# Six score banks instead of four on VectorE in three quads, 128-wide weight reads for B, and B's input transposed in 512-token pieces, in a two-branch attention kernel

## The chip, the cores and the metric

The kernel runs on one core of one Trainium2 chip. Times are device microseconds of that core, given as the median of several executions. Before the change the kernel took 463.41 us (three runs, 463.3 to 463.55). "Faster" or "slower" needs 2%, which is 9.3 us here. Smaller differences are read from ratios with 95% intervals and from the traces.

## The reference

Two attention layers over 2048 tokens of width 448 (16 heads of 28) are computed and set side by side.

```python
def _A_ref(x, wq, wk, wv, wo):            # 16 heads of q, one shared head of k and v
    q = (x @ wq).reshape(B, S, H, Dh).transpose(0, 2, 1, 3)
    k = x @ wk
    v = x @ wv
    scores = einsum("bhqd,bkd->bhqk", q, k) * (Dh ** -0.5)
    p = softmax(scores)
    o = einsum("bhqk,bkd->bhqd", p, v)
    return o.transpose(0, 2, 1, 3).reshape(B, S, H * Dh) @ wo

def _B_ref(x, wqkv, wo):                  # every token sees itself and 7 earlier ones, 2 apart
    # ... q, k, v from x @ wqkv; W, dil = 8, 2
    logits = where(mask, einsum("bhsd,bhswd->bhsw", q, kg) * scale, -1e9)
    o = einsum("bhsw,bhswd->bhsd", softmax(logits), vg)
    return o.transpose(0, 2, 1, 3).reshape(B, S, D) @ wo

return concatenate([a, b], axis=-1)
```

A has 16 x 2048 x 2048 = 67 million exponentials, B next to none. A sets the time, and B's work has to fit beside it.

## The kernel before

A's scores come in 1024 tiles of 128 x 512, each filling one PSUM bank. Sixteen *quads* of 64 tiles follow one another. Two slots of banks take turns: one of three tiles, one of two. ScalarE takes the exponential of a whole slot at once (1536 or 1024 columns). In the quads listed in `OFF_AT`, four rounds of the three-tile slot give their third tile to VectorE, which evicts it and computes the exponential by a polynomial in three passes over two tiles at a time.

```python
SLOTS = ((0, 1, 2), (3, 4))
OFF_AT = {q: (0, 2, 5, 7) for q in range(1, 16)}
OFF_AT.update({q: (0, 1, 3, 4, 6, 7, 9, 10) for q in ()})
# ...
            off = g.offload(n, us)
            na = len(us) - off
            w = 512 * na
            x = a("act", t_exp(w), lambda e, b0=b0, w=w, n=n: e.activation(
                g.expT[:, n % ERING, 0:w], g.ps[:, 512 * b0:512 * b0 + w], ACT.Exp, scale=SCALE),
              R=[("ring", slot)], W=[("expT", n % ERING)], pr=-50)
# ...
    def d_exp(self, bank, slot):
        # ... the eviction, one per tile
        o = a("dve", t_dve_ps(512), lambda e: e.tensor_scalar(
            out=xx[:, 512 * h:512 * h + 512], in0=g.bank(bank), scalar1=-128.0 * A2, scalar2=128.0 * (129 + EOFF),
            op0=ALU.mult, op1=ALU.add), R=[("ring", slot)], W=[("d_x", m % 2, h)], pr=-45)
        # ... then, per two tiles, three scalar_tensor_tensor passes with pr=-0.5
```

`a(engine, duration, emit, R=reads, W=writes, pr=priority, rel=earliest)` only registers an operation. A list scheduler then fixes each engine's order from the registered durations, so a small edit can reorder every engine. The loads that the change touches:

```python
        a("act", 0.5, ...xst <- A_x[0:512]..., W=["xst"], pr=-21)          # first 512 tokens of x, cut here
        a("act", 1.1, wload(g.wk, g.A_wk, 0, DH), W=["wk"], dsem="i_wk", land=3, pr=-20, ninc=2)
        a("sp", 1.1, wload(g.wq, g.A_wq, 0, KC), ..., W=[("wq", 0)], dsem="i_wq0", land=3, pr=-25, ninc=2)
        for c in range(1, NCH):
            for t in range(4):
                a("sp", 1.25, one(lambda e, c=c, t=t: e.dma_start(
                    out=g.xT_A[:, t, 512 * c:512 * c + 512], in_=g.A_x[0, 512 * c:512 * c + 512, XB0[t]:XB0[t] + 128],
                    transpose=True)), W=[("xT", c, t)], dsem=f"i_xa{c}.{t}", land=4.6, pr=-20 + c)
        for t in range(4):
            a("sp", 3.5, one(lambda e, t=t: e.dma_start(
                out=g.xT_B[:, t, :], in_=g.B_x[0, :, XB0[t]:XB0[t] + 128], transpose=True)),
              W=[("xT_B", t)], dsem=f"i_xb{t}", land=8, pr=0, rel=4)
```

B's q and k are computed with weights read `KC` = 112 columns wide, and B's 512 transposing matmuls also take 112-wide operands:

```python
                        g.bank(u.bank, p1=KC), g.wqkv[:, kt, w * D + KC * t:w * D + KC * t + KC],
# ...
                    g.bank(u.bank, 128, 128 * t, p1=KC), g.prod2[:, w, KC * t:KC * t + KC], g.ident[:, :],
```

Of the kernel before, what the change touches and what calls it, by code (L numbers as in the profile page):

```python
# [39 lines left out]
OFF_AT.update({q: (0, 1, 3, 4, 6, 7, 9, 10) for q in ()})  # L40
LATE = 2
DR = 2
# [6 lines left out]
class Op:  # L49
    __slots__ = ("eng", "dur", "emit", "deps", "pr", "rel", "name", "use", "dsem", "land", "nd",  # L50
                 "kids", "start", "end", "seq", "waits", "signal", "count", "vc", "ninc", "claims", "idx",
                 "dense", "fill", "full", "opt", "alone", "lock", "ring", "tiled", "pv")

    def __init__(self, eng, dur, emit, pr, rel, name):
        self.eng, self.dur, self.emit, self.pr, self.rel, self.name = eng, dur, emit, pr, rel, name
        self.deps = set()
        self.use = None
        self.dsem = None
        self.land = 0.0
        self.ninc = 1  # L60
        self.kids = []
        self.start = self.end = None
        self.waits = []
        self.signal = False
        self.claims = None
        self.vc = None
        self.dense = 0.0
        self.fill = None
        self.full = 0
        self.opt = ()  # L70
        self.alone = True
        self.ring = False
        self.tiled = False
        self.pv = False
        self.lock = isinstance(dur, Lock) or (eng == "gp" and emit is not None)
# [16 lines left out]
class Sched:  # L92
# [49 lines left out]
    def run(self, engines):  # L142
# [44 lines left out]
        while left:  # L187
# [5 lines left out]
            if e == "dve":  # L193
                r1 = min((r for (r, o) in cand["dve"] if o.ring), default=None)
                if r1 is not None:
                    n = sum(1 for (_, o) in cand["act"] if o.ring)
                    limit = max(r1, H + (0.9 if n < 1 else 0) - self.QKT - 0.2 - 0.69)
# [33 lines left out]
            if best is None and e == "pe" and self.FILL and T > 4 and (nxt is None or nxt > T + 0.12) and area(T) < self.IDLE:  # L231
# [164 lines left out]
class Gen:  # L396
# [63 lines left out]
    def alloc(self, es):  # L460
# [12 lines left out]
        self.wqkv = sb([128, 4, 2 * D], BF16, "wqkv")  # L473
# [63 lines left out]
    def consts(self):  # L537
# [21 lines left out]
        a("gp", 0.8, lambda e: e.memset(g.wqkv[0:64, 3, :], 0.0), W=["wqkvz"], pr=-8.1)  # L559
# [21 lines left out]
    def loads(self):  # L581
# [11 lines left out]
        a("act", 1.1, wload(g.wk, g.A_wk, 0, DH), W=["wk"], dsem="i_wk", land=3, pr=-20, ninc=2)  # L593
        a("sp", 1.1, wload(g.wq, g.A_wq, 0, KC), R=[("d_x", 0, 0), ("d_x", 0, 1)], W=[("wq", 0)], dsem="i_wq0", land=3, pr=-25, ninc=2)
        a("gp", 1.5, wload(g.wv, g.A_wv, 0, DH), W=["wv"], dsem="i_wv", land=4, pr=-8.3, ninc=2)
        a("gp", 1.5, wload(g.wq, g.A_wq, KC, D), R=[("d_x", 0, 0), ("d_x", 0, 1)], W=[("wq", 1)], dsem="i_wq", land=4, pr=-7.5, ninc=2)
        for c in range(1, NCH):
            for t in range(4):
                a("sp", 1.25, one(lambda e, c=c, t=t: e.dma_start(
                    out=g.xT_A[:, t, 512 * c:512 * c + 512], in_=g.A_x[0, 512 * c:512 * c + 512, XB0[t]:XB0[t] + 128],  # L600
                    transpose=True)), W=[("xT", c, t)], dsem=f"i_xa{c}.{t}", land=4.6, pr=-20 + c)
        for t in range(4):
            a("sp", 3.5, one(lambda e, t=t: e.dma_start(
                out=g.xT_B[:, t, :], in_=g.B_x[0, :, XB0[t]:XB0[t] + 128], transpose=True)),
              W=[("xT_B", t)], dsem=f"i_xb{t}", land=8, pr=0, rel=4)
        a("sp", 1.2, lambda e: [
            e.dma_start(out=g.wqkv[:, 0:3, :], in_=g.B_wqkv[0:384, 0:2 * D].rearrange("(t p) c -> p t c", p=128)),
            e.dma_start(out=g.wqkv[64:128, 3, :], in_=g.B_wqkv[384:448, 0:2 * D]),
            ], W=["wqkv"], dsem="i_wb", land=8, pr=1, rel=4, ninc=2)
# [79 lines left out]
    def a_v(self, c):  # L689

        g, a = self, self.s.add
        pr = c + (0.9 if c else 1.3)
# [27 lines left out]
    def a_q(self, sc, first=False):  # L720
# [3 lines left out]
        for t in range(4):  # L724
            if first:
                pr, rel = (-9.5, 0) if t == 0 else (4.0 + 10 * t, 17.0)
# [28 lines left out]
    def a_loop(self):  # L755
# [6 lines left out]
        pair, late = [], []  # L762
        g.nd = 0
        g.quad = None
        n, pos = -1, 0
        while pos < NU:
# [40 lines left out]
            if off:  # L807
                pair.append((us[na],) + g.d_exp(b0 + na, slot) + (1,))
# [3 lines left out]
            while late and late[0][0] <= n // 2:  # L812
                for x in late.pop(0)[1]:
                    dqs[x[0][:2]][x[0][3]].append(x)
                    if all(dqs[x[0][:2]]):
                        g.pv_group([y.pop(0) for y in dqs[x[0][:2]]])
            for u in us:
                js = quads[u[:2]]
                while all(js):
                    g.pv_group([x.pop(0) for x in js])  # L820

    def pv_group(self, grp):
# [5 lines left out]
        def pv(e):  # L828
            order = [o.seq for o in all_pv]
            first, last = box[0].seq == min(order), box[0].seq == max(order)  # L830
            for (_, _, tb, j), _, src, w in grp:
                x = e.matmul(g.bank(PVBANK, p0=32 * j, p1=32 * j + 32), g.v_aug[:, w, tb, :], src,  # L832
# [9 lines left out]
        all_pv.append(o)  # L842
        if len(all_pv) == 16:
# [11 lines left out]
    def d_exp(self, bank, slot):  # L855
# [11 lines left out]
        o.ring = True  # L867
        if h:
# [4 lines left out]
                out=u, in0=lo, scalar=EP * F, in1=lo, op0=ALU.add, op1=ALU.mult), R=di, W=["d_u"], pr=-0.5)  # L873
            a("dve", t_dve_1x(1024), lambda e: e.scalar_tensor_tensor(  # L874
                out=v, in0=u, scalar=EQ * F * F, in1=lo, op0=ALU.add, op1=ALU.mult), R=["d_u"] + di, W=["d_u"], pr=-0.5)
            a("dve", t_dve_1x(1024), lambda e: e.scalar_tensor_tensor(  # L876
                out=out, in0=v, scalar=EL / F ** 3, in1=xx, op0=ALU.mult, op1=ALU.subtract),
              R=["d_u"] + di, W=[("dexp", m % DR)], pr=-0.5)
        return ("dexp", m % DR), out[:, 512 * h:512 * h + 512].bitcast(BF16)

    def a_quad_end(self, sc, t):
# [5 lines left out]
        for hf in range(hv):  # L887
# [7 lines left out]
            o.deps.update(g.pvs[sc, t])  # L895
# [37 lines left out]
    B0 = 30.0  # L933
# [14 lines left out]
    def b_qk(self, c):  # L948
        g, a = self, self.s.add
        T = g.B0 + g.BSTEP * 4 * c  # L950
        for t in range(4):
            for w in range(2):
# [4 lines left out]
                for kt in range(4):  # L957
                    a("pe", t_mm(512), lambda e, u=u, t=t, kt=kt, w=w: e.matmul(  # L958
                        g.bank(u.bank, p1=KC), g.wqkv[:, kt, w * D + KC * t:w * D + KC * t + KC],
                        g.xT_B[:, kt, 512 * c:512 * c + 512], start=kt == 0, stop=kt == 3),  # L960
                      R=[("xT_B", kt), "wqkv", "wqkvz"], W=[u], use=u, pr=pr, rel=rel, dense=512)
# [4 lines left out]
    def b_v(self, k):  # L966
# [5 lines left out]
        for kt in range(4):  # L972
# [3 lines left out]
              R=[("xT_B", kt), "wqv", "wqvz"], W=[u], use=u, pr=pr, rel=rel, dense=448)  # L976
# [141 lines left out]
```

## Time and profile before

| | before |
|---|---|
| time, median | 463.41 us |
| profiled span | 461.5 us |
| up to the first exponential | 10.94 us |
| first to last exponential | 443.61 us |
| after the last exponential | 6.95 us |
| exponentials on ScalarE | 264 of 1024 columns, 145 of 1536, one of 512 |
| granted clock | 1.00 |

The prediction below shows the busy table, the three stretches and the groups by shape. Four more lines come from the page's table of the costliest groups (line, engine, operation, tiles, shapes, count, then busy us and mean ns of one, then idle time before it and who ended it):

```profile
L800 ACT ACTIVATE expT<-ps 128x1024 bf16<-128x1024 f32 (+1 forms) x410 | 441.7, 1232 | 2.8 <-PE ps L783 2.4
...
L864 DVE TENSOR_SCALAR d_x<-ps 128x512 f32<-128x512 f32 x60 | 41.5, 691 | 39.0 <-PE ps L783 36.8
...
L1059 PE MATMUL ps<-ident,prod 128*112 128x128 bf16 x512 | 43.9, 225 | 0.0
...
L958 PE MATMUL ps<-xT_B,wqkv 128*112 128x512 bf16 x128 | 40.5, 398 | 0.1
```

### The profile page before, as it was taken

The numbers are of one execution on the slowest core, as the hardware profiler recorded it, in microseconds if no ns is written. First come the engines' busy times: TensorE is split into PE (matmuls) and PEld (weight loads), VectorE is DVE, ScalarE is ACT, GpSimd is POOL, SyncE is SP. The second block draws the span as 40 slices with busy tenths as digits, with TensorE's granted clock in tenths as the row PEclk, the third lists the DMA queues.
The fourth block names the chain that finished last, engine by engine and source line by source line (L and its number), as shares of the span: only waits on it lengthen the run. The fifth ranks groups of instructions, "written<-read, shape, count | busy, mean of one in ns | idle before, by whom it ended". The sixth has DMA issues, their size and how long they took to land.

```text
span 461.5 us, 8681 instructions
## 1 busy us (share of the span) xinstructions
PE 422.8 (92%) x3649; PEld 168.2 (36%) x3701; DVE 365.9 (79%) x607; ACT 447.3 (97%) x430; POOL 9.3 (2%) x28
## 2 busy tenths in 40 slices
PE   7889998999998999999989999999899998997995
PEld 2332332333542434334432443334343442443331
DVE  6447888989899796888888688898889878687853
ACT  3999999999999999999999999999999999999994
POOL 7000000000000000000000000000000000000000
PEclk9999999999999999999999999999999999999999
DMA  8991121000401220002201230002200330410001
GB/s 150 164 229 33 48 75 60 11 0 22 161 21 53 89 74 27 1 14 87 91 11 50 81 101 11 12 0 92 86 26 20 111 101 12 136 46 0 11 3 48
DMA packets 41718, 27.34 MB, mean 59 GB/s; under 512 B 17090, under 2 KB 41520, under 8 KB 41680
## 3 DMA queue, kind: packets, MB, share of 16 engines
q1 hardware_dynamic: 40080, 25.35, 19.5%
q0 software_dynamic: 304, 0.73, 0.9%
q10 hardware_dynamic: 1296, 0.71, 0.5%
q8 instruction: 29, 0.48, 0.4%
q14 instruction: 9, 0.07, 0.0%
HBM read 17.60 MB, written 5.52 MB: 50 GB/s over the span
## 4 chain that ended last, share of the span: by engine, by line
ACT 88%; PE 8%; DVE 1%; DMA 1%; issue 0%; ACTq 0%
ACT expT L800 88%; PE ps L783 2%; PE ps L832 1%; PE ps L958 1%; DMA wk<-in_A_wk_dram 1%; PE ps L973 1%; PE ps L781 1%; PE ps L733 1%; PE ps L1059 1%; ACT e_t L1034 0%; PE ps L662 0%; PE ps L917 0%; DVE kT L679 0%; PE ps L747 0%; DVE PV_T L893 0%
## 5 line engine op out<-in xcount | busy, mean ns | idle before, releaser
L800 ACT ACTIVATE expT<-ps 128x1024 bf16<-128x1024 f32 (+1 forms) x410 | 441.7, 1232 | 2.8 <-PE ps L783 2.4
L783 PE MATMUL ps<-qT,kT 32*128 32x512 bf16 x833 | 123.3, 384 | 16.2 <-ACT expT L800 12.9
L832 PE MATMUL ps<-expT,v_aug 128*32 128x512 bf16 x964 | 96.1, 389 | 0.1
L864 DVE TENSOR_SCALAR d_x<-ps 128x512 f32<-128x512 f32 x60 | 41.5, 691 | 39.0 <-PE ps L783 36.8
L783 PEld LDWEIGHTS ps<-qT,kT 32*128 32x128 bf16 x833 | 30.3, 91 | 94.5 <-ACT expT L800 75.3
L781 PE MATMUL ps<-qT,kz 128*128 128x512 bf16 x160 | 50.2, 382 | 10.7 <-ACT expT L800 8.3
L832 PEld LDWEIGHTS ps<-expT,v_aug 128*32 128x32 bf16 x964 | 24.6, 93 | 60.4 <-issue 57.7
L999 DVE TENSOR_TENSOR stage<-qTB,kTB 112x1024 bf16<-112x1024 bf16 x64 | 42.2, 679 | 2.7 <-PE ps L1008 2.7
L1059 PE MATMUL ps<-ident,prod 128*112 128x128 bf16 x512 | 43.9, 225 | 0.0
L1053 DVE TENSOR_TENSOR prod<-Vsh,a_n 128x896 bf16<-128x896 bf16 x64 | 37.8, 616 | 7.2 <-PE ps L1059 7.2
L958 PE MATMUL ps<-xT_B,wqkv 128*112 128x512 bf16 x128 | 40.5, 398 | 0.1
L1059 PEld LDWEIGHTS ps<-ident,prod 128*112 128x112 bf16 x512 | 34.4, 129 | 16.8 <-issue 14.1
L874 DVE SCALAR_TENSOR_TENSOR d_u<-d_u,d_x 128x1024 f32<-128x1024 f32 x30 | 36.4, 1215 | 0.0
L876 DVE SCALAR_TENSOR_TENSOR dexp<-d_u,d_x 128x1024 int16<-128x1024 f32 x30 | 36.4, 1214 | 0.0
L872 DVE SCALAR_TENSOR_TENSOR d_u<-d_x 128x1024 f32<-128x1024 uint16 x30 | 36.3, 1210 | 0.1
L1008 PEld LDWEIGHTS ps<-ones,stage 112*128 112x128 bf16 x512 | 19.4, 96 | 8.4 <-issue 3.2
L1008 PE MATMUL ps<-ones,stage 112*128 112x4 bf16 x512 | 22.1, 167 | 0.0
L781 PEld LDWEIGHTS ps<-qT,kz 128*128 128x128 bf16 x191 | 11.9, 97 | 25.2 <-ACT expT L800 23.1
L958 PEld LDWEIGHTS ps<-xT_B,wqkv 128*112 128x112 bf16 x128 | 14.1, 128 | 16.4 <-issue 11.1
L733 PE MATMUL ps<-xT_A,wq 128*128 128x512 bf16 x57 | 18.3, 383 | 0.6 <-issue 0.3
L1066 PE MATMUL ps<-wo_B,oT 112*128 112x448 bf16 x64 | 18.1, 356 | 0.2 <-DVE oT L1062 0.2
L408 PE MATMUL ps<-warm 128*128 128x512 bf16 x54 | 17.8, 384 | 0.2 <-issue 0.2
(102 smaller groups left out, 302.9 us busy)
## 6 DMA issues: line engine op xcount, KB each, us to landing
Vsh<-v_scratch SPq DMA_DIRECT2D x16, 896.0 KB, 4.7
v_scratch<-Vst SPq DMA_DIRECT2D x16, 112.0 KB, 1.7
out_dram<-outB SPq DMA_DIRECT2D x16, 112.0 KB, 1.7
out_dram<-outA SPq DMA_DIRECT2D x14, 112.0 KB, 1.7
wqkv<-in_B_wqkv_dram SPq DMA_DIRECT2D x1, 672.0 KB, 4.7
stage<-in_A_x_dram ACTq DMA_DIRECT2D x1, 448.0 KB, 4.4
wo_B<-in_B_wo_dram SPq DMA_DIRECT2D x4, 98.0 KB
wo<-in_A_wo_dram SPq DMA_DIRECT2D x4, 98.0 KB
```

The source lines that it names most:

```text
L781: r = e.matmul(g.bank(b0 + i), g.kz[:, j, 128 * tb:128 * tb + 128], g.qT[:, sc % 2, t, :], start=True, stop=True)
L783: r = e.matmul(g.bank(b0 + i), g.kT[32 * j:32 * j + 32, 128 * tb:128 * tb + 128], g.qT[32 * j:32 * j + 32, sc % 2, t, :], start=True, stop ...
L800: x = a("act", t_exp(w), lambda e, b0=b0, w=w, n=n: e.activation(g.expT[:, n % ERING, 0:w], g.ps[:, 512 * b0:512 * b0 + w], ACT.Exp, scale ...
L832: x = e.matmul(g.bank(PVBANK, p0=32 * j, p1=32 * j + 32), g.v_aug[:, w, tb, :], src, start=first, stop=last, tile_position=(0, 32 * j))
L864: o = a("dve", t_dve_ps(512), lambda e: e.tensor_scalar(out=xx[:, 512 * h:512 * h + 512], in0=g.bank(bank), scalar1=-128.0 * A2, scalar2=1 ...
L874: a("dve", t_dve_1x(1024), lambda e: e.scalar_tensor_tensor(out=v, in0=u, scalar=EQ * F * F, in1=lo, op0=ALU.add, op1=ALU.mult), R=["d_u"] ...
L876: a("dve", t_dve_1x(1024), lambda e: e.scalar_tensor_tensor(out=out, in0=v, scalar=EL / F ** 3, in1=xx, op0=ALU.mult, op1=ALU.subtract), R ...
L958: a("pe", t_mm(512), lambda e, u=u, t=t, kt=kt, w=w: e.matmul(g.bank(u.bank, p1=KC), g.wqkv[:, kt, w * D + KC * t:w * D + KC * t + KC], g. ...
L999: op = a("dve", t_dve_2x(1024), lambda e, t=t, qv=qv, kv=kv: e.tensor_tensor(out=g.prodT[0:KC, t, :, :], in0=qv, in1=kv, op=ALU.mult), R=R ...
L1008: r = e.matmul(g.bank(u.bank, 128).rearrange("p (h w) -> p h w", w=WIN)[:, 4 * t:4 * t + 4, w], g.prodT[0:KC, t, w, :], g.ones4[:, :], sta ...
L1053: a("dve", t_dve_2x(2 * D), lambda e, qr=qr, Vv=Vv, av=av: e.tensor_tensor(out=g.prod2[:, 2 * qr:2 * qr + 2, :].rearrange("p w (d h) -> p ...
L1059: a("pe", 0.056, lambda e, u=u, t=t, w=w: e.matmul(g.bank(u.bank, 128, 128 * t, p1=KC), g.prod2[:, w, KC * t:KC * t + KC], g.ident[:, :], ...
```

## The change

It aims at four things: less work for ScalarE (six banks instead of four go to VectorE in quads 5, 9 and 13), faster weight loads for B's q and k (128 wide, over 16 columns of zeros or of the neighbouring weights), the first x alone on the DMA queues (A's transposes wait for it), and tokens of B that arrive in pieces (16 transposes of 512 tokens instead of 4 of 2048), so that B starts earlier (`B0` 30 to 22). VectorE's three passes get a higher priority. Some registered durations and priorities change too, of the B weights' load among others. The core of the diff, with the scheduler's bookkeeping cut:

```diff
-OFF_AT.update({q: (0, 1, 3, 4, 6, 7, 9, 10) for q in ()})
+OFF_AT.update({q: (0, 2, 3, 5, 7, 8) for q in (5, 9, 13)})
 LATE = 2
+PSTT = -1.5
 # ... (the limit for VectorE's other work is now taken per eviction, from the exponential beside it)
-        self.wqkv = sb([128, 4, 2 * D], BF16, "wqkv")
+        self.wqkv = sb([128, 4, 2 * D + 16], BF16, "wqkv")
 # ...
-        a("act", 1.1, wload(g.wk, g.A_wk, 0, DH), W=["wk"], dsem="i_wk", land=3, pr=-20, ninc=2)
-        a("sp", 1.1, wload(g.wq, g.A_wq, 0, KC), R=[("d_x", 0, 0), ("d_x", 0, 1)], W=[("wq", 0)], dsem="i_wq0", land=3, pr=-25, ninc=2)
+        a("sp", 1.1, wload(g.wk, g.A_wk, 0, DH), W=["wk"], dsem="i_wk", land=3, pr=-25, ninc=2)
+        a("act", 1.1, wload(g.wq, g.A_wq, 0, KC), R=[("d_x", 0, 0), ("d_x", 0, 1)], W=[("wq", 0)], dsem="i_wq0", land=3.2, pr=-20, ninc=2)
 # ... A's transposes
-                    transpose=True)), W=[("xT", c, t)], dsem=f"i_xa{c}.{t}", land=4.6, pr=-20 + c)
-        for t in range(4):
-            a("sp", 3.5, one(lambda e, t=t: e.dma_start(
-                out=g.xT_B[:, t, :], in_=g.B_x[0, :, XB0[t]:XB0[t] + 128], transpose=True)),
-              W=[("xT_B", t)], dsem=f"i_xb{t}", land=8, pr=0, rel=4)
+                    transpose=True)), R=["xst"], W=[("xT", c, t)], dsem=f"i_xa{c}.{t}", land=3.8, pr=-20 + c)
+        for c in range(NCH):
+            for t in range(4):
+                a("sp", 1.05, one(lambda e, c=c, t=t: e.dma_start(
+                    out=g.xT_B[:, t, 512 * c:512 * c + 512], in_=g.B_x[0, 512 * c:512 * c + 512, XB0[t]:XB0[t] + 128],
+                    transpose=True)), W=[("xT_B", c, t)], dsem=f"i_xb{c}.{t}", land=4.5, pr=-16 + c)
 # ... P x V groups for the two tiles that do not fill a group of four; small priorities
-            ... scalar_tensor_tensor passes ..., pr=-0.5)
+            ... scalar_tensor_tensor passes ..., pr=PSTT)
-    B0 = 30.0
+    B0 = 22.0
 # ...
-                        g.bank(u.bank, p1=KC), g.wqkv[:, kt, w * D + KC * t:w * D + KC * t + KC],
-                        g.xT_B[:, kt, 512 * c:512 * c + 512], start=kt == 0, stop=kt == 3),
-                      R=[("xT_B", kt), "wqkv", "wqkvz"], W=[u], use=u, pr=pr, rel=rel, dense=512)
+                        g.bank(u.bank), g.wqkv[:, kt, w * D + KC * t:w * D + KC * t + 128],
+                        g.xT_B[:, kt, 512 * c:512 * c + 512], start=kt == 0, stop=kt == 3),
+                      R=[("xT_B", c, kt), "wqkv", "wqkvz", "wqkve"], W=[u], use=u, pr=pr, rel=rel, dense=512)
```

## The prediction

> **What bounds the kernel now.** I read four views of the profile of the kernel before: the busy table and the 40 slices, the chain of work that ended last, the groups by shape, and the timelines of the first 28 us and the last 16 us. The busy table and the chain name the same engine:
>
> ```profile
> PE 422.8 (92%) x3649; PEld 168.2 (36%) x3701; DVE 365.9 (79%) x607; ACT 447.3 (97%) x430; POOL 9.3 (2%) x28
> ...
> ACT  3999999999999999999999999999999999999994
> ...
> ACT 88%; PE 8%; DVE 1%; DMA 1%; issue 0%; ACTq 0%
> ```
>
> ScalarE (ACT) is full in every slice but the first and the last, and is 88% of the chain. TensorE shows 92% too, but that is overlapped latency: a score matmul is booked at 384 ns, while three cost 0.39 us together. So the span has three terms: the head up to the first exponential, ScalarE's exponentials with whatever gaps lie between them, and the tail after the last one.
>
> The busy time in three stretches, cut at the first and after the last exponential (length, then busy us of PE, PEld, DVE, ACT, POOL, clock, DMA share, GB/s):
>
> ```profile
> 0.00:10.94 10.94, 8.29 (x41) 2.99 (x41) 6.56 (x23) 3.77 (x7) 8.45 (x24) 1.00 0.78 150
> 10.94:454.55 443.61, 411.75 (x3595) 164.32 (x3646) 355.86 (x575) 442.55 (x422) 0.83 (x4) 1.00 0.20 57
> 454.55:461.50 6.95, 2.81 (x16) 0.89 (x14) 3.50 (x10) 0.98 (x2) 0.00 (x0) 1.00 0.20 66
> ```
>
> In the middle ScalarE idles 443.61 - 442.55 = 1.06 us. No order of the other engines can gain more than that there; only fewer exponentials can. The groups by shape give their price:
>
> ```profile
> L800 ACT ACTIVATE expT<-ps 128x1024 bf16<-128x1024 f32 x264 | 267.9, 1084 | 0.3 <-PE ps L781 0.2
> L800 ACT ACTIVATE expT<-ps 128x1536 bf16<-128x1536 f32 x145 | 218.3, 1506 | 2.5 <-PE ps L783 2.4
> ```
>
> One score tile (512 columns) more costs 1506 - 1084 = 422 ns. The first exponential's own wait is 1.74 of the 2.5 us. The timeline of ScalarE shows most of the rest in one place:
>
> ```profile
> 10.94 6.07 ACT L800 ACTIVATE expT<-ps 128x1536 bf16<-128x1536 f32 x5 [1.74 <-PE ps L783]
> ...
> 25.49 3.71 ACT L800 ACTIVATE expT<-ps 128x1536 bf16<-128x1536 f32 x3 [0.65 <-PE ps L783]
> ```
>
> The 0.65 us is the wait for the third 512 tokens of k (the chain has VectorE's kT at 24.24 to 25.00 just before).
>
> **What the Trainium skill says.** "Trainium Kernel Development and Optimization", NeuronCore Architecture, gives ScalarE 1.2 GHz; at one column a cycle 512 columns are 427 ns, and the measured 422 agrees. "TensorE: Matmul & The Clock Gate", Weight-path perf modes, says the fast weight load is on when the number of weights is 128 and the type is not FP32. The trace agrees: weight loads of 112 columns for B's q and k take 128 ns, those of 128 columns 95 to 98 ns. "DMA: Bandwidth & Descriptors", Issuing engines are not separate DMA queues, says all queues end on the same 16 DMA engines and interleave. The trace agrees: a 512-token transpose lands 3.8 us after its issue when little else moves, and 6.8 us when GpSimd's loads of wq and B's v weights are in flight.
>
> **The change, part by part.**
>
> 1. *Three quads with six banks on VectorE.* Each of the other quads gives VectorE four score tiles, quad 0 none: 60 now. Quads 5, 9 and 13 give six: 66. The order of instructions confirms it: 264 to 270 exponentials of 1024 columns, 145 to 139 of 1536, the total of 410 unchanged. ScalarE saves 6 x 0.427 = 2.56 us, all on the path. VectorE pays 6 evictions x 0.69 + 3 x 3 passes x 1.21 = 15.0 us. Its 365.9 becomes some 381 of 461 us, so on average it is no bound. In such a quad (some 27 us) it has 3 x (3.64 + 1.38) = 15.1 us of exponential work beside about 14 us of other work (my estimate: 365.9 less 151 of offload and head, over 16 quads). That is 29 in 27 us, so B's work slips out of these quads. The passes now go first, so what slips isn't what ScalarE waits for. Cost to the span here: 0, but B ends later (part 4).
>
> 2. *128-wide weights.* 128 loads lose some 30 ns each: 128 x 0.03 = 3.9 us of TensorE's weight time over the whole run. TensorE does not set the 1.06 us of idle, so 0 on the path.
>
> 3. *The loads.* x's transposes of A now wait for the first 512 tokens of x, so that these are alone. But in the built order three of the new B transposes, which wait for nothing, stand ahead of them on SyncE's queue, so the queue isn't alone at all. SyncE issues one 512-token transpose in 1.26 us, a pace of 15.58/12 = 1.30 us:
>
> ```profile
> 1.94 15.58 SPq L599 DMA_TRANSPOSE xT_A<-in_A_x_dram  x12
> ...
> 17.56 10.18 SPq L603 DMA_TRANSPOSE xT_B<-in_B_x_dram  x4
> ```
>
>    The three take from 1.94 to 5.8 us, x has landed by then (TensorE took it at 5.23), and A's transposes start at 5.8 instead of 1.94. The four that make tokens 512 to 1023 are then the fourth to seventh in line. I asked the trace one transpose at a time: the one issued at 8.4 landed 6.8 us later, at 15.2, and the one issued at 9.7 landed 6.3 us later, at 16.0. The DMA engines were over 90% busy between 4 and 16 us, so a landing is set by the work queued, which is the same in kind and place in the new kernel. Estimate: the last of the four lands at 16.0. In the new order of TensorE, its k matmul stands *before* the scores of tiles 10 to 12. In the kernel before, these tiles' exponential (the fifth) started at 10.94 + 4 exponentials = 15.5 (it ends at 17.0 and takes 1.5). In the new one: 16.0 + 0.2 for the matmul + 0.3 for five small v matmuls + 0.4 for the scores = 17.0. That is **+1.5 us**, whatever the head gains in front of it. In front I expect little: wk comes earlier (it was the last to land, at 6.4), but wq takes its place behind x on the other queue. The second link, kT of these tokens (copy 0.68, square 0.42, matmul 0.4, add 0.75 after 16.4) is ready at about 19.0 and the scores that need it are wanted about then, so at most 0.1 more. Tokens 1024 to 1535 are then no longer late, for ScalarE has been pushed back and their transposes land by about 19.4 (issued by 14.9 in the trace before): the old 0.65 us goes, **-0.65**.
>
> 4. *The tail.* Before, B is done at 449 and the end is A's last projection alone:
>
> ```profile
> 448.42 0.62 DVE L1069 CAST outB<-ps 128x448 bf16<-128x448 f32 x1 [1.89 <-PE ps L1066]
> ...
> 457.71 1.16 DVE L927 CAST outA<-ps 128x448 bf16<-128x448 f32 x2
> ```
>
>    In the new order B's last block is still open: ten of its transposing matmuls stand after A's last exponentials on TensorE, and on VectorE its oT copy stands between the last oTn transposes and the outA copies, its outB copy at the very end. By the old times: oTn ends at 457.6, oT copy 0.6 to 458.2, four projection matmuls 0.93 (what A's last four took) to 459.2, outB 0.6 to 459.9. Before, the last copy ended at 457.71 + 1.16 = 458.87. The store takes as long as before, so **+1.1 us**.
>
> Sum: 463.41 - 2.56 + 1.5 - 0.65 + 1.1 = **462.8 us**.
>
> **Rivals.**
>
> - *The author's intent holds:* k arrives in time (the transposes land at 14.5 or sooner, because B's early ones or the missing wq on SyncE's queue change the backlog) and the tail hides in the store. Then 463.4 - 2.56 - 0.65 - some 0.4 of head = 459.8. For it: the first exponential waits on wk today (the chain has 4.48 us of wk's DMA). Against it: SyncE's pace of 1.30 us and its queue order are plain, and B's last copies are in the path by order.
> - *VectorE becomes the bound in quads 5, 9 and 13.* Each late eviction holds the next scores of that slot and so ScalarE; one pass in the way is 1.2 us. If two evictions per dense quad meet one, that is 3 x 2 x 1.2 = 7 us and a time of 470. For it: 29 us of work in 27. Against it: in the trace before ScalarE never waits for VectorE in the middle although the same rule places the evictions, and the passes' 1.21 us is what the placing reckons with.
> - *The delayed loads hurt more than once:* SyncE now ends its loads some 10 us later (16 short transposes at 1.3 us against 4 long ones in 10.2). B's first q matmul stands after 60 score tiles, near 38 us by the pace of 2.28 us for five; its weights and tokens land by about 27. So I give this up to 1.5 us, 464.3.
>
> **Range and chances.** The stall at k is uncertain by 0.8 us either way, the tail by 0.6, leftover idle by 0.4, and dense quads only upwards; the first rival pulls downwards. I take 460.2 to 464.8. Faster by 2% would need under 454.1, more than all the head, idle and exponentials named here can give: 0.01. Slower by 2% needs 472.7, only the second rival doubled: 0.02. Within 2%: 0.97.
>
> **What would show it right or wrong.** Right: 1024-column exponentials x270 and some 2.5 us less busy on ScalarE; a gap of 1 to 2 us before the fifth exponential, released by scores that stood behind the k matmul, the last landing of these four transposes near 16 us; no gap near 25 us; VectorE's last instruction an outB copy, about 7 to 8 us after the last exponential. Wrong: no such gap (then the transposes are faster than the trace before says); waits of ScalarE for scores released by VectorE's d_x in quads 5, 9, 13; or an e_t activation waiting for VectorE.

## More of the kernel before

410 exponentials of 1232 ns are 505 us, but their busy time is 441.7 us. The booked times therefore overlap by 63 us, or 0.15 us each.

## The result, and the profile after

The changed kernel took **461.04 us** (median of four runs, 460.78 to 461.35), beside 463.36 us (463.26 to 463.55) for the kernel before in the same rounds. A ratio here is the mean time of one kernel's runs over that of the other's of the same rounds, so it is not quite the ratio of the medians quoted. Executions over 1.5% slower than the fastest of the same kernel are left out of the means. It is 0.995, interval 0.9933 to 0.9967: by the 2% rule "same", in fact 2.3 us faster. All runs were at a granted clock of 1.00. The prediction was 462.8 us, so it lies inside the range, but 1.8 us too high.

The same three stretches of the changed kernel (length, then busy us of PE, PEld, DVE, ACT, POOL, clock, DMA share, GB/s):

```profile
0.00:11.29 11.29, 9.07 (x42) 3.97 (x42) 6.86 (x23) 3.77 (x6) 8.58 (x25) 1.00 0.75 154
11.29:451.72 440.43, 414.40 (x3613) 157.71 (x3612) 369.28 (x588) 440.18 (x422) 0.80 (x4) 1.00 0.20 57
451.72:459.20 7.48, 4.27 (x30) 1.90 (x28) 4.57 (x12) 0.98 (x2) 0.00 (x0) 1.00 0.24 77
```

| stretch | before | after | difference | predicted |
|---|---|---|---|---|
| up to the first exponential | 10.94 | 11.29 | +0.35 | 0 |
| first to last exponential | 443.61 | 440.43 | -3.18 | -1.71 |
| after the last exponential | 6.95 | 7.48 | +0.53 | +1.1 |
| span | 461.5 | 459.2 | -2.3 | -0.6 |

The middle gave 1.5 us more than predicted. Its parts in the groups by shape:

```profile
L806 ACT ACTIVATE expT<-ps 128x1024 bf16<-128x1024 f32 x270 | 269.7, 1066 | 0.1
L806 ACT ACTIVATE expT<-ps 128x1536 bf16<-128x1536 f32 x139 | 207.2, 1490 | 2.0 <-PE ps L789 1.9
```

The counts are the predicted ones, 270 and 139. Their means fell too, from 1084 to 1066 ns and from 1506 to 1490 ns, although the shapes are the same; why is not settled, and the reading below goes by the starts, not by these durations.

The timeline of ScalarE at the start (start, length, engine, line, operation, count, idle before) shows no stall:

```profile
11.29 5.97 ACT L806 ACTIVATE expT<-ps 128x1536 bf16<-128x1536 f32 x5 [1.90 <-PE ps L789]
...
17.19 7.84 ACT L806 ACTIVATE expT<-ps 128x1024 bf16<-128x1024 f32 x7
...
24.89 6.98 ACT L806 ACTIVATE expT<-ps 128x1536 bf16<-128x1536 f32 x6
```

Five exponentials run without a printed gap from 11.29 to 17.26, so the predicted stall of 1 to 2 us before the fifth is absent. The old 0.65 us near 25 is gone, as predicted.

SyncE's timeline shows that the order of the loads was read rightly:

```profile
1.94 3.86 SPq L608 DMA_TRANSPOSE xT_B<-in_B_x_dram  x3
5.84 16.61 SPq L603 DMA_TRANSPOSE xT_A<-in_A_x_dram  x12
...
23.66 17.51 SPq L608 DMA_TRANSPOSE xT_B<-in_B_x_dram  x13
```

Three transposes of B go first, and A's start at 5.84. The last of the four that the fifth exponential needs is the fourth of A's, now the **seventh in SyncE's queue**. It was issued at 9.75 and landed at 14.1, 4.4 us after its issue. The seventh in the queue before (the seventh of A's, for later tokens), from which the prediction took its 16.0, landed 6.3 us after an issue at 9.74.

The end of the timeline, after the last exponential at 451.72:

```profile
453.99 0.76 DVE L923 STREAM_TRANSPOSE oTn<-oN 128x256 bf16<-128x256 bf16 x2
...
454.67 0.65 DVE L1082 CAST oT<-ps 112x512 bf16<-112x512 f32 x1
...
455.25 1.14 DVE L947 CAST outA<-ps 128x448 bf16<-128x448 f32 x2
...
455.38 0.93 PE L1086 MATMUL ps<-wo_B,oT 112*128 112x448 bf16 x4
...
456.35 0.62 DVE L1089 CAST outB<-ps 128x448 bf16<-128x448 f32 x1
```

B's last block is closed inside A's tail, as predicted, and the last copy is outB, ending at 456.97. That is 5.25 us after the last exponential. Before, the last copy (outA) ended at 458.87, 4.32 us after the last exponential at 454.55. So this chain grew by 0.93 us (predicted 1.1; the prediction's own addends, from 457.6 to its outB, give 459.7 to 459.8, so 0.9). The last store, however, needed 459.20 - 456.97 = 2.23 us instead of 461.50 - 458.87 = 2.63 us, which leaves +0.53.

### The profile page after: what moved, and what is told of

Its sections match the earlier page's. It is cut to its first block, busy times and chain, and to the rows that moved or that the text cites. A ratio compares the mean times of both kernels' runs of the same rounds, so it can differ in the third digit from the quotient of the medians.

```text
span 459.2 us, 8717 instructions
## 1 busy us (share of the span) xinstructions
PE 427.7 (93%) x3682; PEld 163.6 (36%) x3682; DVE 380.7 (83%) x622; ACT 444.9 (97%) x430; POOL 9.4 (2%) x29
## 4 chain that ended last, share of the span: by engine, by line
ACT 86%; PE 11%; DVE 1%; DMA 1%; issue 0%
ACT expT L806 85%; PE ps L789 2%; PE ps L1079 2%; PE ps L850 2%; PE ps L787 1%; DMA stage<-in_A_x_dram 1%; PE ps L978 1%; PE ps L1086 1%; PE ps L937 1%; ACT e_t L1054 0%; PE ps L654 0%; PE ps L738 0%; PE ps L1028 0%; PE ps L434 0%; PE ps L993 0%
## 5 line engine op out<-in xcount | busy, mean ns | idle before, releaser
L787 PE MATMUL ps<-qT,kz 128*128 128x512 bf16 x200 | 59.6, 383 | 9.9 <-ACT expT L806 9.4
L883 DVE TENSOR_SCALAR d_x<-ps 128x512 f32<-128x512 f32 x66 | 45.4, 688 | 17.9 <-PE ps L789 16.8
L1079 PE MATMUL ps<-ident,prod 128*112 128x128 bf16 x512 | 41.8, 224 | 0.0
L894 DVE SCALAR_TENSOR_TENSOR d_u<-d_u,d_x 128x1024 f32<-128x1024 f32 x33 | 40.1, 1215 | 0.1
L896 DVE SCALAR_TENSOR_TENSOR dexp<-d_u,d_x 128x1024 int16<-128x1024 f32 x33 | 40.0, 1213 | 0.1
L892 DVE SCALAR_TENSOR_TENSOR d_u<-d_x 128x1024 f32<-128x1024 uint16 x33 | 39.9, 1209 | 0.2
L1079 PEld LDWEIGHTS ps<-ident,prod 128*112 128x112 bf16 x512 | 34.2, 130 | 14.7 <-issue 10.9
L978 PE MATMUL ps<-xT_B,wqkv 128*128 128x512 bf16 x128 | 38.9, 383 | 0.0
L993 PE MATMUL ps<-wqv,xT_B 128*128 128x448 bf16 x64 | 17.5, 356 | 0.0
L913 DVE STREAM_TRANSPOSE PV_T<-ps 128x512 f32<-128x512 f32 (+1 forms) x17 | 11.4, 676 | 6.7 <-PE ps L850 6.5
```

Of the source, the lines that this page charges most:

```text
L787: r = e.matmul(g.bank(b0 + i), g.kz[:, j, 128 * tb:128 * tb + 128], g.qT[:, sc % 2, t, :], start=True, stop=True)
L883: o = a("dve", t_dve_ps(512), lambda e: e.tensor_scalar(out=xx[:, 512 * h:512 * h + 512], in0=g.bank(bank), scalar1=-128.0 * A2, scalar2=1 ...
L892: a("dve", t_dve_1x(1024), lambda e: e.scalar_tensor_tensor(out=u, in0=lo, scalar=EP * F, in1=lo, op0=ALU.add, op1=ALU.mult), R=di, W=["d_ ...
L894: a("dve", t_dve_1x(1024), lambda e: e.scalar_tensor_tensor(out=v, in0=u, scalar=EQ * F * F, in1=lo, op0=ALU.add, op1=ALU.mult), R=["d_u"] ...
L896: a("dve", t_dve_1x(1024), lambda e: e.scalar_tensor_tensor(out=out, in0=v, scalar=EL / F ** 3, in1=xx, op0=ALU.mult, op1=ALU.subtract), R ...
L978: a("pe", t_mm(512), lambda e, u=u, t=t, kt=kt, w=w: e.matmul(g.bank(u.bank), g.wqkv[:, kt, w * D + KC * t:w * D + KC * t + 128], g.xT_B[: ...
```

## The experiments

Twelve kernels ran. Except where said, each is the changed kernel with one edit. "Middle" is the time from the start of the first exponential to the end of the last. Three sets of kernels ran on three chips, so times are compared inside a set, or by the ratio to the kernel before, which ran in each. A profile shows one execution of several, and not always a typical one. The open questions were these: which part of the change gives the 3.2 us in the middle, why did the stall not come, and is VectorE near its limit?

| run | first exponential at | middle | time, median | ratio to before |
|---|---|---|---|---|
| set 1: e1_four | 10.92 | 442.35 | 462.26 | 0.9978 (0.9965 to 0.9991) |
| e2_w112 | 10.93 | 442.18 | 462.11 | 0.9975 (0.9962 to 0.9988) |
| e4_xalone | 10.93 | 440.42 | 460.97 | 0.9969 (0.9942 to 0.9997) |
| d0_before | 11.30 | 443.61 | 463.66 (one run) | |
| set 2: e9_prod128 | 11.06 | 439.73 | 460.01 | 0.9923 (0.9909 to 0.9937) |
| e6_pst | 10.87 | 439.72 | 460.08 | 0.993 (0.9916 to 0.9943) |
| e3_nowait | 10.93 | 440.42 | 460.67 | 0.994 (0.9926 to 0.9954) |
| e7_six_a | 11.20 | 436.63 | 475.47 | 1.026 (1.0245 to 1.0275) |
| set 3: a2_after | 11.10 | 440.57 | 460.88 | 0.994 (0.9926 to 0.9954) |
| e5_swapback | 11.19 | 440.42 | 461.53 | 0.9955 (0.9937 to 0.9974) |
| b1_pst_pad | 11.07 | 439.94 | 462.65 | 0.9967 (0.9937 to 0.9997) |
| b2_b18_pad | 10.64 | 447.08 | 466.08 | 1.0045 (1.0028 to 1.0062) |

### e1_four: four banks in every quad

```diff
-OFF_AT.update({q: (0, 2, 3, 5, 7, 8) for q in (5, 9, 13)})
+OFF_AT.update({q: (0, 2, 3, 5, 7, 8) for q in ()})
```

> The changed kernel with four offloaded score tiles in quads 5, 9 and 13 as in all others, all else of the change kept. Theory (the banks are the gain): 6 exponentials grow by 512 columns, 6 x 0.427 = 2.56 us more of ScalarE; B's last block is done before A's last exponential, as before the change, so the tail is some 0.5 us shorter: 461.0 + 2.56 - 0.5 = 463.1 us. Rival (the loads and the head are the gain, and the six tiles cost VectorE what they save ScalarE): 461.0 or below.

Measured: 462.26 us (462.07 to 463.37, six runs), middle 442.35.

```profile
10.92:453.27 442.35, 415.93 (x3632) 159.72 (x3631) 357.80 (x575) 441.76 (x422) 0.80 (x4) 1.00 0.20 57
```

The six extra banks are therefore worth 442.35 - 440.43 = 1.92 us of the middle, less than the 2.56 predicted. In quads 5, 9 and 13 the step is 0.87, 0.70 and 0.89, together 2.46 us, nearly the price of the columns; the other thirteen quads are together 0.54 us slower with the six banks. Of that, 0.17 is the last exponential, booked at 0.761 us instead of 0.593; the rest is spread in small pieces over a changed order. After the last exponential e1_four needs 7.03 us, the changed kernel 7.48, so 1.5 us of the 1.92 remain in the span counted from the first exponential. And with no extra bank, the middle is still 443.61 - 442.35 = 1.26 us shorter than before. That 1.26 exceeds the 1.06 us of idle that the prediction called the most there was to gain, although 442.35 - 441.76 = 0.59 us of printed idle is still there.

### e2_w112: B's q and k weights 112 wide again

```diff
-                        g.bank(u.bank), g.wqkv[:, kt, w * D + KC * t:w * D + KC * t + 128],
+                        g.bank(u.bank, p1=KC), g.wqkv[:, kt, w * D + KC * t:w * D + KC * t + KC],
```

The order on every engine is exactly that of the changed kernel, so this is a pure change of width. The matmuls themselves are booked with it, at 397 ns instead of 383; the run gives the worth of the width and not of the weight load alone.

> The changed kernel with B's q and k weights read 112 wide again; the order of all instructions on every engine is the same as in the changed kernel. Theory (TensorE doesn't set the end): weight loads 128 ns instead of 97, the same time within 0.3 us, 461.0. Rival (TensorE is at its limit in the stretches where the chain runs through it): 128 x 0.03 = 3.9 us of weight loading come back in part as gaps before exponentials, 462 to 464 us.

Measured: 462.11 us (461.82 to 462.89, six runs). "Worth nothing" has fallen; the rival of 462 to 464 held. The 128 weight loads take 128 ns instead of 97 (the changed kernel's line first):

```profile
L978 PEld LDWEIGHTS ps<-xT_B,wqkv 128*128 128x128 bf16 x128 | 10.4, 97 | 16.9 <-issue 10.2 <-DVE d_u L894 0.2 <-DVE oN L920 0.2
...
L978 PEld LDWEIGHTS ps<-xT_B,wqkv 128*112 128x112 bf16 x128 | 14.5, 128 | 15.7 <-issue 10.2 <-DVE d_u L894 0.2 <-DVE outB L1089 0.2
```

The middle is 1.75 us longer. Not all of it is the width: the timeline of ScalarE has a gap at the start that the changed kernel did not have.

```profile
10.93 4.63 ACT L806 ACTIVATE expT<-ps 128x1536 bf16<-128x1536 f32 x4 [1.90 <-PE ps L789]
16.05 1.45 ACT L806 ACTIVATE expT<-ps 128x1536 bf16<-128x1536 f32 x1 [0.48 <-PE ps L789]
```

It stands before the fifth exponential, where the prediction had put its stall, and here the fourth of A's transposes landed at 15.1. That is before any of B's q and k weights is used, at 38.35. Counted from the exponential just after that first use (from 39.18 us, and from 38.83 in the changed kernel), the rest of the middle is 413.93 us against 412.89: the width is worth **1.04 us** on the path. The profiled run is the slowest of the six.

### Where a wait hides on a busy engine

How can weights matter when ScalarE's printed idle in the middle is 1.06 us before and 440.43 - 440.18 = 0.25 us after? The starts of the exponentials answer it. Fed in time, a 1024-column exponential is followed by the next after 0.903 us and a 1536-column one after 1.330 us; the median intervals in both traces are within 0.001 us of these. The booked durations of the kernel before are never below 1.018 and 1.445 us. So an exponential is booked at least 0.115 us past the start of a successor that comes in time, and a wait up to that length prints as busy time. The durations hardly tell it either: a 1024-column one in the kernel before is booked 1.083 us on average where its successor was in time, and 1.097 us where it came over 0.05 us late.

Summed over all exponentials, the intervals exceed 0.903 and 1.330 us by this much (the few other instructions of ScalarE taken off, by the trace 0.306 us for each of B's eight exponentials and 0.054 us for each of four small copies):

| | waits in the middle, printed and hidden |
|---|---|
| before | 9.1 us |
| changed kernel | 8.3 us |
| e1_four | 7.8 us |
| e2_w112 | 10.1 us |
| e9_prod128 | 7.6 us |

In the kernel before, about 7.8 of the 9.1 us stand where a score matmul had ended (by the profile's modelled ends) less than 0.06 us before the exponential started, so it was most likely waiting for TensorE. After, it is about 6.7 of 8.3. Why these scores came late, because of other work on TensorE or because VectorE's evictions freed a bank late, was not separated. In the changed kernel the 66 exponentials whose slot VectorE had helped to empty waited 41 ns each, the other 138 of three-tile slots 22 ns.

The Trainium skill, "Perfetto Trace Analysis", Identifying the Most-Contended Engine, says that for Scalar the occupancy percentage is also a fair measure of how close you are to roofline. Here 442.55 of 443.61 us was 99.8% occupancy, with 9.1 us of waits inside. The measure is therefore fair to about 2%, which is more than all the gains at stake here, and the measurement decides.

### e9_prod128: the same cure for 512 more weight loads

If TensorE's weight loads cost hidden waits, B's 512 transposing matmuls should gain from it too. They still load 112 columns at 130 ns, as the changed kernel's line shows:

```profile
L1079 PEld LDWEIGHTS ps<-ident,prod 128*112 128x112 bf16 x512 | 34.2, 130 | 14.7 <-issue 10.9 <-DVE outB L1089 0.5 <-DVE d_x L883 0.2
```

```diff
-        self.prod2 = sb([128, WIN, D], BF16, "prod2")
+        self.prod2 = sb([128, WIN, D + 16], BF16, "prod2")        # the 16 columns set to zero once
-                    g.bank(u.bank, 128, 128 * t, p1=KC), g.prod2[:, w, KC * t:KC * t + KC], g.ident[:, :],
+                    g.bank(u.bank, 128, 128 * t), g.prod2[:, w, KC * t:KC * t + 128], g.ident[:, :],
```

> The changed kernel with one more set of weights read 128 wide: the 512 loads of B's products (112 wide, 130 ns each in the profile), by padding each row of the products with 16 zero columns; the order of instructions stays that of the changed kernel. Theory (ScalarE's small waits, hidden by the overlap of its instructions, come from TensorE's late scores, so TensorE time does move the end): 512 x 0.03 = 15 us less weight loading, of which perhaps a tenth sits in front of late scores, as with B's q and k weights (3.9 us of loading gave 1.0): 1 to 2.5 us faster than the changed kernel, 459 to 460 us. Rival (only the idle that the profile prints counts, and that is 0.25 us): 461.0.

Measured: 460.01 us (459.77 to 460.04, five runs). The loads became faster and the middle shorter:

```profile
L1079 PEld LDWEIGHTS ps<-ident,prod 128*128 128x128 bf16 x512 | 30.0, 98 | 15.2 <-issue 11.1 <-DVE outB L1089 0.3 <-DVE qT L748 0.2
```

```profile
11.06:450.79 439.73, 413.36 (x3613) 154.14 (x3612) 369.44 (x588) 439.52 (x422) 0.80 (x4) 1.00 0.20 57
```

The middle is 439.73, 0.70 us under the changed kernel's, whose printed idle there was only 0.25 us: the rest of the gain came out of hidden waits. Four times as many loads gave less than the 128 did, so the gain does not go by the sum of the loads. It should depend on which of them stand just before a wanted score matmul; that was not tested. On the same chip, e3_nowait (the changed kernel but for SyncE's queue) took 460.57 to 461.0, so all five runs here lie below all four of those. By the median this is the **fastest version** (e6_pst, 460.08, is level with it), and it beats both kernels.

### e4_xalone and e3_nowait: what the order of the loads is worth

In e4_xalone B's transposes wait for x as well, so that x is truly alone. Only SyncE's queue changes.

```diff
-                    transpose=True)), W=[("xT_B", c, t)], dsem=f"i_xb{c}.{t}", land=4.5, pr=-16 + c)
+                    transpose=True)), R=["xst"], W=[("xT_B", c, t)], dsem=f"i_xb{c}.{t}", land=4.5, pr=-16 + c)
```

> The changed kernel with B's transposes waiting for the first x as well, so that x is really alone; only SyncE's queue changes (A's twelve transposes, then B's sixteen), the order on the other engines is the same. Theory (x was nearly alone before, its data ran from 3.0 to 4.4 us, and the k matmul's transposes land in time already): x lands at most 0.3 us earlier, the first exponential moves by less than 0.3 us, the time stays at 461.0 within 0.4. Rival (the three transposes delay x and wq): first exponential 0.5 to 1 us earlier, 460.2.

Measured: 460.97 us (460.49 to 464.18, six runs), middle 440.42, the same as the changed kernel's to 0.01 us. A's transposes start at 4.78, x lands 4.0 us after its issue (4.0 in the changed kernel, 4.4 before), and the fourth of A's transposes lands at 14.2. Four of its six runs lie between 460.49 and 461.2; the other two took 463.56 and 464.18, at a clock of 0.996, and were not profiled.

In e3_nowait A's transposes go first and wait for nothing, as before the change. The other engines' orders are untouched, because the dependency is dropped only after the ordering.

```diff
             self.s.run(engines)
+            # drop x's load from what the transposes of A and B wait for
             self.s.resolve(engines)
-                    transpose=True)), W=[("xT_B", c, t)], ...
+                    transpose=True)), R=["xst"], W=[("xT_B", c, t)], ...   # so that they are ordered behind A's
```

> The changed kernel with SyncE's queue as before the change: A's twelve transposes at once after wk, without the wait for the first x, then B's sixteen; the order of the other engines is that of the changed kernel. Theory (the order of the loads gains nothing): the seventh-landing problem is gone as the four transposes come first, and the time is 461.0 within 0.5. Rival (the wait lets x land sooner and that is worth something): x lands 0.3 us later or more and the first exponential too, 461.5.

Measured: 460.67 us (460.57 to 461.0, four runs), middle 440.42 again. So with x alone, nearly alone, or not at all, the middle is the same and the first exponential starts at 10.93 to 11.29. That part of the change gained nothing that can be measured here.

### d0_before: the kernel before, profiled again

> The kernel before once more, for a second profile of its head. If the landing of transposes is the program's own, the one issued at 9.7 us lands at 16.0 again and the one issued at 8.4 at 15.2; if it varies from run to run by a microsecond or more, my prediction's 16.0 was one draw. Likewise TensorE's 16 transposes of x: 1.07 us again, or 1.9 us as in the changed kernel's profile, if that was the clock still held back at the start.

Measured: span 461.9, first exponential at 11.30 instead of 10.94, middle 443.61 as in the first profile, the seventh transpose of the queue landing at 15.9. The head of one and the same program moves by 0.36 us, so the +0.35 of the changed kernel's head is not an effect of the change. The middle does not move.

### a2_after: the changed kernel again

> The changed kernel once more, as the yardstick of this call and for a second profile of its head. Expected: 461.0 within 0.4; the stretch from first to last exponential 440.4 us again (in the runs so far it repeats to 0.02 us when the orders are the same and k is in time); the first exponential anywhere from 10.9 to 11.3; the last of the four transposes at 14.1 to 15.2 us.

Measured: 460.88 us (460.77 to 461.27, five runs), middle 440.57. The fourth of A's transposes landed at 14.7 here and 14.1 the first time; quad 0 is 0.15 us longer, the whole difference of the middle.

### e5_swapback: is the swap of wk and wq what lands the transposes early?

Behind x on ScalarE's queue wk stands again, and wq goes first on SyncE's; their places are exchanged after the ordering.

```diff
             self.s.run(engines)
+            # wk and wq's first columns exchange their engines and places in the queues
             self.s.resolve(engines)
```

> The changed kernel with wk behind x on ScalarE's queue and wq first on SyncE's, as before the change; the order of the other engines is unchanged. Theory (this swap is what makes the seventh transpose land 1 to 2 us sooner than in the kernel before, by leaving fewer rows between x and the transposes): the seventh lands at 15.7 to 16.1, a gap of about 1.2 us before the fifth exponential, and the time is 462.0. Rival (landing varies by itself): 14.1 to 15.2 again, 461.0.

Measured: 461.53 us (460.83 to 462.59, four runs), middle 440.42. In the profiled run the transpose landed at 14.4 and there is no gap. That run is the fastest of the four by time. The spans of all four are 459.1, 459.1, 459.4 and 460.8 us, beside 459.0 to 459.5 in a2_after, so only one of them leaves room for the late landing that was expected (a time of 462.0). The theory that the swap alone brings the landing forward has not held.

Two things have to be kept apart. The *seventh in the queue*, issued at 9.74 or 9.75, landed at 16.0 and 15.9 in the two profiles of the kernel before and at 14.8 in e3_nowait; in these it is the seventh of A's, and the fourth of A's (issued at 5.84) had landed at 9.7, 8.7 and 9.3. In the changed order the seventh is the fourth of A's: 14.1, 14.7 (a2), 14.2 (e1), 15.1 (e2), 14.5 (e9), 14.3 (e6), 14.6 (e7) and 14.4 (e5). With x alone the fourth of A's is the fourth in the queue, issued at 8.6 to 8.7, and landed at 14.2 (e4), 15.7 (b1) and 15.9 (b2). So the same order of SyncE's queue gives landings up to 1.8 us apart.

The fifth exponential follows the fourth of A's: no printed gap up to 14.7, then gaps of 0.48 us at 15.1, 0.94 at 15.7 and 1.59 at 15.9. In these three it starts 0.92 to 0.93 us after the landing (the prediction had added 1.0). What makes the landing vary stays open; the order of the loads and the swap of the weights were each undone alone, never both together.

### e6_pst: the passes without their priority

```diff
-PSTT = -1.5
+PSTT = -0.5
```

> The changed kernel with the old priority of VectorE's passes (not first); the orders shift on every engine. Theory (the place of the passes matters little, a late offloaded tile doesn't hold ScalarE; B's work runs a little earlier): 461 within 0.8 us. Rival (passes first is what keeps the six-bank quads free of stalls): gaps in quads 5, 9 and 13, 462.5 or more.

Measured: 460.08 us (459.89 to 460.7, five runs), middle 439.72:

```profile
10.87:450.59 439.72, 416.12 (x3628) 157.92 (x3628) 370.64 (x588) 439.41 (x422) 0.80 (x4) 1.00 0.20 57
```

The higher priority was not needed for the six-bank quads: without it the table of printed waits still shows no exponential of A waiting for VectorE, and the middle is 0.7 us shorter in the trace. The timed runs overlap with those of e3_nowait on the same chip (460.57 to 461.0), so as a gain it is small and not secured.

### e7_six_a: six banks in six quads

```diff
-OFF_AT.update({q: (0, 2, 3, 5, 7, 8) for q in (5, 9, 13)})
+OFF_AT.update({q: (0, 2, 3, 5, 7, 8) for q in (3, 5, 7, 9, 11, 13)})
```

> The changed kernel with six offloaded tiles in six quads (3, 5, 7, 9, 11, 13) in place of three. Theory of the banks alone: 6 x 0.427 = 2.56 us less again, 458.4. My theory (VectorE is near its limit: 381 + 15 = 396 us of work, and what slips of B ends after A): ScalarE's last exponential some 2 us earlier, but B's last block, half done at the end already with three quads, is a block or more behind, and the tail grows by 8 to 18 us: 468 to 476.

Measured: 475.47 us (475.26 to 475.93, four runs), 2.6% slower than before, as expected.

```profile
11.20:447.83 436.63, 408.26 (x3461) 150.33 (x3460) 372.03 (x579) 436.46 (x421) 0.80 (x4) 1.00 0.19 56
447.83:473.30 25.47, 19.65 (x216) 12.25 (x214) 16.48 (x36) 1.39 (x3) 0.00 (x0) 1.00 0.14 46
```

ScalarE finishes 3.9 us sooner (447.83 against 451.72), and its exponentials still don't print a wait for VectorE. But VectorE could not do B's blocks beside it, and 25.47 us of them are left for the end. VectorE's limit shows as a backlog behind the last exponential and not as a wait in the middle.

### b1_pst_pad and b2_b18_pad: do the gains add?

b1_pst_pad has e4's, e6's and e9's edits together. b2_b18_pad is b1 with

```diff
-OFF_AT.update({q: (0, 2, 3, 5, 7, 8) for q in (5, 9, 13)})
+OFF_AT.update({q: (0, 2, 3, 5, 7, 8) for q in (4, 8, 12)})
-    B0 = 22.0
+    B0 = 18.0
```

> The changed kernel with three of the findings together: passes not first, products' weights 128 wide, B's transposes behind A's. If the gains add (0.7 of each of the first two in the stretch of exponentials): 439.0 us from first to last exponential, 459.4 in time. If both fill the same gaps: 439.7 and 460.0.

> As b1, with B's work released 4 us earlier and the six-bank quads at 4, 8 and 12: another order with the same number of offloaded tiles. Theory (the order decides only the small waits, which lie between 7.5 and 8.5 us in all orders so far): 459 to 460.5. Rival (B done earlier shortens the tail by the 0.5 us that the changed kernel lost): 458.9.

Measured for b1: 462.65 us, six runs from 460.25 to 468.1. One of them, the 468.1, is slow (clock 0.982); the five others still spread from 460.25 to 464.43, so in time no gain over e9 or e6 alone is shown. The profiled run is the fastest. Its middle, 439.94, is no shorter than theirs, but it contains the late landing, a gap of 0.94 us. Counted from the exponential at which e2_w112 was compared, after that gap, 411.22 us remain. The changed kernel has 412.89 there, e9 and e6 412.18 each. So the two gains, 0.71 us each, do add in that stretch (to 1.67 us), and what comes before it, the late landing above all, takes 1.2 us of that back.

```profile
11.07 4.63 ACT L806 ACTIVATE expT<-ps 128x1536 bf16<-128x1536 f32 x4 [1.90 <-PE ps L789]
16.64 1.45 ACT L806 ACTIVATE expT<-ps 128x1536 bf16<-128x1536 f32 x1 [0.94 <-PE ps L789]
```

Measured for b2: 466.08 us (464.99 to 466.96, six runs; the profiled one is the slowest), slower than before by 0.45%, and its middle has 15.0 us of waits. A third of that is one stall, shown by the timeline of all engines around 54 us:

```profile
50.41 0.39 SPq L626 DMA_DIRECT2D v_scratch<-Vst  x1
53.84 0.62 DVE L997 CAST Vst<-ps 128x448 bf16<-128x448 f32 x1 [6.19 <-DMA v_scratch<-Vst]
...
54.52 0.61 PE L738 MATMUL ps<-xT_A,wq 128*128 128x512 bf16 x1 [4.61 <-DVE Vst L997]
...
55.72 2.52 ACT L806 ACTIVATE expT<-ps 128x1536 bf16<-128x1536 f32 x2 [5.11 <-PE ps L789]
```

Read it from the bottom: ScalarE waited 5.11 us for scores, TensorE's wq matmul ahead of these scores waited 4.61 us for VectorE's copy of B's v to clear a bank, VectorE's copy waited 6.19 us for a small DMA that still read that buffer, and that DMA was issued at 50.41, because it stands on SyncE's queue behind the sixteen short transposes of B and eight small loads of output weights. In the kernel before it was issued at 35.13, in the changed one at 46.46, in b1_pst_pad at 48.88. In b1, VectorE's copy waited only 1.53 us for it and ScalarE did not stall, so the queue is not all of it: b2 also calls for B's work 4 us earlier. TensorE's clock also fell after its pause: the wq matmul takes 0.61 us instead of 0.39. The Trainium skill, "TensorE: Matmul & The Clock Gate", What's actually happening, says that a gate halves the clock after an idle window of about 3.4 us. The trace agrees: TensorE's printed idle is 4.61 us, and the granted clock from 54 to 60 us is 0.50. All six runs of b2 have a mean clock of 0.993. Four runs of b1 and e4 (463.56 to 464.43) have 0.993 to 0.996, so a pause of this kind may have struck there too; no profile of them was kept.

## Why the prediction was right or wrong

**The head, 0: right.** +0.35 us measured, but the kernel before varies by 0.36 on its own (d0_before), and the new orders start anywhere from 10.64 to 11.29.

**Six banks, -2.56: the mechanism is right, the size a little large.** The quads concerned are shorter by 2.46, and 0.54 of it is given back elsewhere, 0.17 by the longer last exponential and the rest as small waits, leaving 1.92 (e1_four).

**128-wide weights, 0 on the path: wrong.** e2_w112 measures 1.04 us. The step of the prediction that failed is "In the middle ScalarE idles 443.61 - 442.55 = 1.06 us. No order of the other engines can gain more than that there". The true waits were 9.1 us, mostly for TensorE's scores, because booked exponentials overlap by 0.115 us and more. The same fence that I quoted gave the means that should have stopped me: 264 x 1.084 + 145 x 1.506 = 504.5 us of booked time in a stretch of 443.61.

**The stall at k, +1.5: wrong in size, by all of it.** "A landing is set by the work queued, which is the same in kind and place in the new kernel" is the failed step. The seventh transpose of the queue landed 4.4 us after its issue and not 6.3. The chain from a late landing to the gap is right: e2, b1 and b2 show gaps of 0.48, 0.94 and 1.59 us at landings of 15.1, 15.7 and 15.9. It was the landing that could not be read from one trace. Why the seventh landed at 16 in both profiles of the kernel before, and near 14.4 in most of the new order, is not settled; neither the wait for x (e3) nor the swap of the weights (e5) explains it alone.

**The old gap near 25 us, -0.65: right.** It is gone in every profile of the new order.

**The tail, +1.1: right in kind.** The chain grew by 0.93; the last store was 0.40 shorter, so +0.53.

**Sum.** The middle fell by 3.18. By experiments that is 1.92 for the banks and 1.04 for the weights; the remaining 0.2 was not measured apart: the old gap of 0.65 is in it, and other changes of order. By the starts of the exponentials it is 6 x (1.330 - 0.903) = 2.56 for fewer columns and 9.1 - 8.3 = 0.8 less waiting, less 0.17 for the last exponential, which is booked longer: together 3.2. The total came inside the range partly by its width (4.6 us): the two wrong terms, 1.5 for the stall and 1.04 for the weights, both made the prediction too high, the tail did so too, and only the head and the overrated banks worked the other way.

**The rivals.** The first (k in time, tail partly hidden; 459.8) came nearest in its mechanism, and in its number too (1.2 us off, against 1.8). The second (VectorE as the bound) did not occur, and where it was provoked (e7_six_a) it took another form: a backlog at the end. The third (delayed loads) did not occur in the changed kernel but did in b2_b18_pad, through a small DMA that nobody had thought of as a load.

## What to carry to other kernels

Before writing "the bound engine is idle for only so long", compare count times mean with busy time: if the booked times overlap, take the shortest interval from start to start as the price, and the sum over it as the waiting. Work on an engine off the chain can then be worth something, if it stands in front of what feeds the bound engine. A landing read from one trace is good to a microsecond or two, so give a stall that hangs on it a range and not a number; and look at what stands last on a queue before putting more transfers ahead of it.

## What the Trainium skill lacked or had wrong

- "Perfetto Trace Analysis", Identifying the Most-Contended Engine: occupancy as a fair measure for Scalar. ScalarE was 99.8% occupied in the middle and still had 9.1 us of 443.6 in waits, so the measure is off by 2%. Exponentials booked at 1.018 and 1.445 us at least follow each other every 0.903 and 1.330 us. That booked times of instructions in a row overlap is in the skill; that a wait inside the overlap prints as busy time is not.
- "TensorE: Matmul & The Clock Gate", Weight-path perf modes: the condition of 128 weights holds, but the measured gain it gives, about twice, is not what the profile books here for one load: 128 to 97 ns and 130 to 98 ns, or 1.3 times (booked durations; the rate of loads in a row was not measured). It also does not say that reading 128 columns where only 112 are used earns it, which it does (1.04 us and 0.70 us of the middle).
- The same page, What's actually happening, calls the start of the clock gate run-variable, and the runs fit that: TensorE's sixteen transposes of x took 1.07 us in the kernel before, e1, e5 and e9, and 1.80 to 1.89 us in the changed kernel and most others. The profile prints a granted clock of 1.00 over both heads, so that the clock is the cause is not shown. The first exponential did not start later for it: 10.93 in e4_xalone with the slow ones, 10.94 before with the fast.
- "DMA: Bandwidth & Descriptors", DMA Transpose (X-bar): no issue cost or landing time for a transpose of 512 tokens x 128 columns. The runs show 1.3 us of SyncE each, and landings 2.6 to 7.3 us after issue over A's twelve.
- No page says how far landings vary from run to run in the same queue order: 14.1 to 15.1 us in the changed order, 14.2 to 15.9 with x alone, for the fourth of A's.
